# Two pairs of batches share one inverse iteration, and both head groups share what follows their scores

## The chip, the cores and the metric

The kernel runs on one core of a Trainium2 chip. The metric is the device time of one execution in microseconds (us); lower is better. The core has five engines with queues of their own: TensorE (PE in the profile, its weight loads PEld), VectorE (DVE), ScalarE (ACT), GpSimd (POOL) and SyncE (SP), which here issues all the DMAs.

## The reference

The kernel computes a Nystrom attention over 8 batches of 8 heads, 576 tokens and 64 channels, and a gated MLP on its output (4608 tokens, width 512, hidden width 1536). Everything is float32.

```python
q_lm, k_lm = means of q and k over 18 neighbouring tokens   # 32 landmarks per head
A  = sm(q, k_lm)        # 576 x 32
Bm = sm(q_lm, k_lm)     # 32 x 32
C  = sm(q_lm, k)        # 32 x 576
Z = Bm.T / (norm1(Bm) * norminf(Bm) + 1e-06)
for _ in range(6):
    Z = 2 * Z - Z @ Bm @ Z
attn = A @ Z @ C @ v
x = attn as (4608, 512);  xn = x / rms(x) * rms_g
out = (silu(xn @ w_gate) * (xn @ w_val)) @ w_out
```

`sm` is a scaled softmax over the last axis. The six steps of the iteration on Z depend on one another.

## The kernel before, in words

A float32 product is made from high and low parts: a large matmul of the MLP becomes three (high by high, high by low, low by high). The 8 heads of a batch are two groups `g` of four heads; a group fills the 128 partitions with four blocks of 32 landmarks.

**Attention, per batch b.** `stage1(b, g)` (line 335) sums q and k over 18 tokens (lmT, line 342), issues the loads of the next group's q and k and of its v (lines 347 and 348), and makes the scores sC, sA and B with small matmuls, their softmax for C and B (E, eb, Bm) and the transposed scores tA (line 395). `back()` (line 404), one for each group, follows some units later: the softmax of A on tA (lines 405 to 414), the transposed result AT and its parts AS, five transposes of E on TensorE (sE, sF), their copies ET and EL, and 20 small matmuls pCV of C by v, scaled into PV. `newton(b)` (line 459) does the inverse iteration for both groups of one batch: some preparation on DVE, p0 (8 matmuls of 32x32 blocks), five steps of pn (8 matmuls each) followed by one DVE instruction (line 498), a sixth pn into VZ (line 502), and pW (8 matmuls), split into Whi and Wlo. Steps carry Z and Z C v together. `second(b)` (line 539) multiplies W by AS (pO, 12 matmuls a group), copies pO into xr on ACT and squares it (sq), sums the squares with matmuls (pss, transposed on DVE, then pms), takes the reciprocal root with small DVE instructions (lines 571 to 581), spreads it (Rb, Rt), scales xr (line 587), stores xr to DRAM for the later passes (line 591), and `finish` splits xr into xhi and xlo (lines 614 and 616).

**MLP.** Tokens go in chunks of 512. `mlp_chunk(i)` (line 252) runs 144 large matmuls on the first four of twelve blocks of the hidden width: for each block 12 into psg and 12 into psv, silu and the product into h, then pso. The other eight blocks follow in two later passes over all tokens. A chunk of 512 tokens is not a batch of 576: chunk i needs x of batch i (its last part in `finish(i - 1, 1)`) before its first matmul.

**What sets the order.** All matmuls and transposes are held in program order, and a planner, `Mixer` (line 212), writes that order. Each piece of attention is a generator that yields a cost and a due time: `yield cost, wait` moves the planner's clock by the cost and makes the piece due again after wait times slack (1.3 once chunk 0 has begun). `fill` (line 239) moves the clock by 0.216 for each MLP matmul and then runs at most one due piece of attention. After the 144 matmuls of chunk i, `drain` (line 244) runs what is left, with no MLP matmul between, until `second(i + 1)` is done (line 690). Pieces start when their gates open (lines 638 to 660): `newton(b)` when the scores of b are done, and its steps after both `back()` of b; `second(b)` when newton(b) is done and chunk b - 1 has begun; the second half of `stage1(b)` when `second(b - 2)` is done, its first half when `newton(b - 2)` is. Chunks 7 and 8 and the later passes come after all attention. On the other engines a scheduler orders instructions by priority; `second` and `newton` go first.

**Buffers that the change touches.** PSUM has eight banks: three for the MLP, five (`pa`) for attention. E and tA have two buffers (one per group), xr has two, v two.

Of the kernel before, what the change touches and what calls it, by code (L numbers as in the profile page):

```python
# [18 lines left out]
P = 128  # L19
# [10 lines left out]
BW = 5.0  # L30
# [19 lines left out]
TAB = 2  # L50
# [25 lines left out]
TINY = 1.0513759e-09  # L76


@with_exitstack
def nystrom_moe_kernel(  # L80
# [47 lines left out]
    VZ = cst.tile([P, G, 3 * D], F32, name="VZ")  # L128
# [169 lines left out]
    with tc.tile_pool(name="ap", bufs=1, side="right") as ap, tc.tile_pool(  # L298
# [36 lines left out]
        def stage1(b, g):  # L335
            nt = state[b]
            qk = loaded.pop((b, g))
            vt, vl_ = loaded.pop((b, g, "v"))
# [7 lines left out]
            if b > 0 and nxt[0] < B:  # L346
                load_qk(*nxt)
                load_v(*nxt)
# [25 lines left out]
            rs = sm.tile([P, 2], F32, name="rs", tag="rs")  # L374
# [5 lines left out]
            E = ap.tile([P, S], F32, name="E", tag="E", bufs=2)  # L380
# [11 lines left out]
            (nc.scalar.mul if BMA else nc.vector.tensor_scalar_mul)(nt["Bm"][:, g, :], eb, rs[:, 1:2])  # L392
            tA = ap.tile([P, NB, M], F32, name="tA", tag="tA", bufs=TAB)
            for e in range(2):
                nc.vector.transpose(
                    tA[:, e * (NB // 2) : (e + 1) * (NB // 2), :].rearrange("p n m -> p (n m)"),
                    sA[e],
                )
            yield 1.3, 0.0
            if g == 1:  # L400
                stage["front"] = b

            def back():
                yield -BW * mix.slack
                mA = sm.tile([P, NB], F32, name="mA", tag="mA")
                nc.vector.tensor_reduce(mA, tA, axis=AX.X, op=ALU.max)
                nc.gpsimd.tensor_sub(tA, tA, mA.unsqueeze(2).broadcast_to([P, NB, M]))
                nc.scalar.activation(tA, tA, AF.Exp, scale=SC)
                sumA = sm.tile([P, NB], F32, name="sumA", tag="sumA")
                nc.vector.tensor_reduce(sumA, tA, axis=AX.X, op=ALU.add)  # L410
                nc.vector.tensor_scalar_add(sumA, sumA, 1e-9)
                rA = sm.tile([P, NB], F32, name="rA", tag="rA")
                nc.vector.reciprocal(rA, sumA)
                nc.gpsimd.tensor_mul(tA, tA, rA.unsqueeze(2).broadcast_to([P, NB, M]))
                AT = ap.tile([P, S], F32, name="AT", tag="AT", bufs=ATB)
                nc.vector.transpose(AT, tA.rearrange("p n m -> p (n m)"))
                AS = ap.tile([P, 2, S], F32R, name="AS", tag="AS", bufs=ASB)
                nc.scalar.copy(AS[:, 0], AT)
                nc.vector.tensor_sub(AS[:, 1], AT, AS[:, 0].bitcast(F32))
                nt["AT"][g] = AS  # L420

                sE = pa.tile([P, 4, P], F32, name="sE", tag="pa")
                for ch in range(4):
                    tp(sE[:, ch], E[:, ch * P : (ch + 1) * P], ident)
                sF = pa.tile([2 * M, P], F32, name="sF", tag="pa")
                tp(sF, E[:, 4 * P :], ident)
                ET = ap.tile([P, 4, P], F32, name="ET", tag="ET", bufs=ETB)
                EL = ap.tile([2 * M, P], F32, name="EL", tag="EL", bufs=ETB)
                nc.scalar.copy(ET, sE)
                nc.scalar.copy(EL, sF)  # L430
                yield 0.65, SW2
                pCV = pa.tile([P, D], F32, name="pCV", tag="pa")
                for ch in range(5):
                    for h in range(4):
                        r = slice(h * M, (h + 1) * M)
                        mm(
                            pCV[r, :],
                            ET[:, ch, r] if ch < 4 else EL[:, r],
                            vt[:, h, ch, :] if ch < 4 else vl_[:, h, :],
                            start=(ch == 0),  # L440
                            stop=(ch == 4),
                        )
                (nc.scalar.mul if CVA else nc.vector.tensor_scalar_mul)(nt["PV"][:, g, M:], pCV, rs[:, 0:1])
                yield 0.85, 0.2
                done[b] = done.get(b, 0) + 1
                if done[b] == 2:
                    stage["first"] = b

            mix.add(back())

        def bmm(lt, rhs, n, nm):
            ps = pa.tile([P, 2, n], F32, name=nm, tag="pa")
            for g in range(2):
# [5 lines left out]
        def newton(b):  # L459
            nt = state[b]  # L460
            Bm = nt["Bm"]
            BT = sm.tile([P, 2, M], F32, name="BT", tag="BT", bufs=1)
# [3 lines left out]
            sums = sm.tile([P, 4], F32, name="nsum", tag="nsum")  # L466
            nc.vector.tensor_reduce(
                sums[:, 0:2], Bm, axis=AX.X, op=ALU.add, apply_absolute_value=True
            )
            nc.vector.tensor_reduce(  # L470
                sums[:, 2:4], BT, axis=AX.X, op=ALU.add, apply_absolute_value=True
            )
            sb = sm.tile([P, 4, M], F32, name="nsb", tag="nsb", bufs=1)
            nc.vector.tensor_copy(sb, sums.unsqueeze(2).broadcast_to([P, 4, M]))
            sbt = sm.tile([P, 4, M], F32, name="nsbt", tag="nsbt", bufs=1)
# [3 lines left out]
            nm = sm.tile([P, 4], F32, name="nnm", tag="nnm")  # L479
            nc.vector.tensor_reduce(nm, sbt, axis=AX.X, op=ALU.max)  # L480
            den = sm.tile([P, 2], F32, name="nden", tag="nden")
            nc.vector.tensor_mul(den, nm[:, 0:2], nm[:, 2:4])
            nc.vector.tensor_scalar_add(den, den, 1e-6)
            nc.vector.reciprocal(den, den)
            Bs = sm.tile([P, 2, M], F32, name="Bs", tag="Bs")
            nc.vector.tensor_mul(Bs, Bm, den.unsqueeze(2).broadcast_to([P, 2, M]))
            PV = nt["PV"]
            yield 0.0, NW
            p0 = bmm(BT, BT, M, "p0")
            nc.vector.tensor_mul(PV[:, :, :M], p0, den.unsqueeze(2).broadcast_to([P, 2, M]))  # L490
            yield 0.35, 0.0
            while stage["first"] < b:
                yield -0.3
            yield 0.0, NS
            for _ in range(5):
                pn = bmm(PV[:, :, :M], PV, M + D, "pn")
                PVn = sm.tile([P, 2, M + D], F32, name="PV", tag="PV", bufs=3)
# [5 lines left out]
                VZ[:, :, D : 2 * D], PV[:, :, M:], 2.0, pn, op0=ALU.mult, op1=ALU.subtract  # L503
            )
            yield 0.45, NP
            Whi = sm.tile([P, 2, P], F32R, name="Whi", tag="Whi", bufs=1)
            Wlo = sm.tile([P, 2, P], F32R, name="Wlo", tag="Wlo", bufs=1)
            pW = pa.tile([P, 2, P], F32, name="pW", tag="pa")
            for g in range(2):
# [12 lines left out]
            nt["W"] = Whi, Wlo  # L522
            yield 0.5, WW

        def new_state(b):
            state[b] = {
                "Bm": sm.tile([P, 2, M], F32, name="Bm", tag="Bm"),
                "PV": sm.tile([P, 2, M + D], F32, name="PV", tag="PV", bufs=3),
                "AT": [None, None],
            }  # L530

        def first(b):
            new_state(b)
            for g in range(2):
                yield from stage1(b, g)
# [3 lines left out]
        def second(b):  # L539
            nt = state.pop(b)  # L540
            (Whi, Wlo), ATs = nt["W"], nt["AT"]
            xr = ap.tile([P, NK, S], F32, name="xr", tag="xr", bufs=2)
# [511 lines left out]
```

## Time and profile before

| | us |
|---|---|
| median of 3 runs (1065.81 to 1072.3) | 1068.71 |
| the profiled execution's own time | 1064.71 |
| its span, first to last instruction | 1062.8 |
| TensorE busy | 992.8 |
| DVE busy | 743.4 |
| ACT busy | 486.7 |
| POOL busy | 89.5 |

The profile is of one execution. Its busy times are sums over instructions, where pipelined matmuls overlap and their ends are modelled. A name such as `psg<-xhi,whig` gives the tile written and the tiles read, with buffer numbers left out. All matmuls carry line 141 (the helper `mm`) and the transposes line 144, so they are told apart by tile. A note in brackets after an instruction gives the idle time of its engine just before it and what ended it. The granted clock is that of TensorE, as a share of full speed.

### The profile page before, as it was taken

The page shows a single profiled execution, that of the slowest core. Times are in us where ns is not written, and L with a number is a line of the kernel's source. Part 1 is how long each engine was busy: PE and PEld are TensorE (multiplying, and loading weights), DVE is VectorE, ACT ScalarE, POOL GpSimd, SP SyncE. Part 2 cuts the span into 40 slices and gives each one's busy share as a digit, 9 for nine tenths or more (in the row PEclk, how much of TensorE's full clock was granted, in tenths as well). Part 3 has the DMA queues.
Part 4 walks back from the last instruction along what each step waited for, and adds up shares of the span by engine and source line. Part 5 has one row for each costly group of instructions (what it writes and reads, how often), then busy time and mean ns, then how long its engine had stood idle before and what let it go on. Part 6 is the DMA issues. An engine that isn't in the chain of part 4 may idle for free.

```text
span 1062.8 us, 17582 instructions
## 1 busy us (share of the span) xinstructions
PE 992.8 (93%) x6918; PEld 833.9 (78%) x6918; DVE 743.4 (70%) x1503; ACT 486.7 (46%) x990; POOL 89.5 (8%) x86
## 2 busy tenths in 40 slices
PE   5639689989989999999999999999999999999998
PEld 3326466556767777787989899998999989899997
DVE  7799586797494551988995675747897475675743
ACT  3534556555454543455645352433744334352431
POOL 2243121211020210100000000000000000000000
PEclk7659889999999999999999999999999999999999
DMA  9244343434140211543533505134250432505122
GB/s 335 100 150 136 133 164 105 153 104 163 43 142 11 86 45 40 187 145 119 189 123 135 178 1 179 51 129 155 64 178 21 159 96 83 179 1 178 50 70 80
DMA packets 62946, 123.82 MB, mean 117 GB/s; under 512 B 5520, under 2 KB 27024, under 8 KB 61840
## 3 DMA queue, kind: packets, MB, share of 16 engines
q1 hardware_dynamic: 62864, 122.71, 34.0%
q8 instruction: 54, 0.88, 0.3%
q14 instruction: 28, 0.23, 0.1%
HBM read 84.94 MB, written 37.75 MB: 115 GB/s over the span
## 4 chain that ended last, share of the span: by engine, by line
PE 72%; DVE 15%; DMA 6%; issue 2%; ACT 2%; POOL 2%; SPq 0%; ACTq 0%; POOLq 0%; DVEq 0%
PE pso L141 23%; PE px L141 18%; PE pz L141 9%; PE psg L141 6%; PE psv L141 5%; PE pw L141 5%; DMA qk<-in_q_dram 2%; PE pO L141 2%; DMA srawv<-in_moe_w_val_dram 1%; DVE lmT L342 1%; PE pn L141 1%; DVE xr L587 1%; DVE h L275 1%; PE sC L141 1%; PE pss L141 1%
## 5 line engine op out<-in xcount | busy, mean ns | idle before, releaser
L141 PE MATMUL pso<-whio,h 128*128 128x512 f32 x288 | 96.2, 402 | 5.8 <-DVE h L275 4.7
L141 PE MATMUL pso<-solo,h 128*128 128x512 f32 x432 | 100.4, 390 | 0.0
L829 ACT CAST x<-xf 128x768 fp32r<-128x768 f32 x84 | 68.1, 833 | 69.7 <-DVE xf L847 54.2
L141 PEld LDWEIGHTS pso<-solo,h 128*128 128x128 f32 x432 | 81.0, 188 | 16.3
L141 PE MATMUL pso<-sowhio,h 128*128 128x512 f32 x288 | 90.9, 390 | 0.0
L141 PE MATMUL psg<-xhi,whig 128*128 128x512 f32 x144 | 60.7, 421 | 25.6 <-ACT xhi L614 25.6
L945 DVE TENSOR_TENSOR ob<-ob,pso 128x512 f32<-128x512 f32 x72 | 48.8, 684 | 49.1 <-PE pso L141 48.1
L830 DVE TENSOR_TENSOR x<-xf,x 128x768 fp32r<-128x768 f32 x84 | 79.2, 953 | 5.0 <-ACT x L829 5.0
L877 DVE TENSOR_TENSOR h<-c,h 128x384 fp32r<-128x384 f32 x96 | 53.2, 555 | 37.3 <-ACT h L876 37.2
L898 ACT COPY c<-px 128x384 f32<-128x384 f32 x48 | 23.1, 481 | 108.6 <-PE px L141 108.6
L141 PEld LDWEIGHTS pso<-whio,h 128*128 128x128 f32 x288 | 53.4, 188 | 20.4 <-DVE h L275 6.0
L876 ACT CAST h<-c 128x384 fp32r<-128x384 f32 x96 | 49.4, 515 | 34.5 <-DVE c L887 28.3
L141 PE MATMUL psg<-xlo,whig 128*128 128x512 f32 x144 | 60.6, 421 | 4.7 <-DVE xlo L616 4.0
L141 PEld LDWEIGHTS pso<-sowhio,h 128*128 128x128 f32 x288 | 54.1, 188 | 11.0
L141 PE MATMUL psg<-xhi,wlog 128*128 128x512 f32 x144 | 60.5, 420 | 0.0
L141 PE MATMUL psv<-xhi,wlov 128*128 128x512 f32 x144 | 58.1, 403 | 0.0
L141 PE MATMUL px<-x,swfs0c 128*128 128x384 f32 x288 | 58.0, 335 | 0.0
L141 PE MATMUL psv<-xlo,whiv 128*128 128x512 f32 x144 | 58.0, 403 | 0.0
L141 PE MATMUL px<-x,swfs1c 128*128 128x384 f32 x288 | 57.8, 334 | 0.1
L141 PE MATMUL px<-x,swfs2c 128*128 128x384 f32 x288 | 57.8, 335 | 0.0
L141 PE MATMUL psv<-xhi,whiv 128*128 128x512 f32 x144 | 57.8, 401 | 0.0
L141 PE MATMUL pso<-wloo,h 128*128 128x512 f32 x144 | 57.4, 398 | 0.0
(224 smaller groups left out, 2231.6 us busy)
## 6 DMA issues: line engine op xcount, KB each, us to landing
xd<-xr SPq DMA_DIRECT2D x8, 1152.0 KB, 4.3
pd<-ob SPq DMA_DIRECT2D x36, 256.0 KB, 2.1
xf<-xd SPq DMA_DIRECT2D x8, 1152.0 KB, 7.5
ob<-pd SPq DMA_DIRECT2D x36, 256.0 KB, 3.5
pe<-ob SPq DMA_DIRECT2D x36, 256.0 KB, 2.6
ob<-pe SPq DMA_DIRECT2D x36, 256.0 KB, 2.8
out_dram<-ob SPq DMA_DIRECT2D x36, 256.0 KB, 2.7
vt<-in_v_dram SPq DMA_DIRECT2D x16, 512.0 KB, 4.0
```

The costliest lines, as they stand in the source:

```text
L141: tc.keep_in_program_order(nc.tensor.matmul(*args, **kw))
L275: nc.vector.tensor_sub(h2, s, h1.bitcast(F32))
L342: nc.vector.tensor_reduce(lmT[:, z], qk[z].rearrange("p h (m c) -> p h m c", c=LM), axis=AX.X, op=ALU.add)
L587: last = nc.vector.scalar_tensor_tensor(xr[:, kk], xr[:, kk], gsb[:, kk : kk + 1], Rt, op0=ALU.mult, op1=ALU.mult)
L829: nc.scalar.copy(t[:, 0], src)
L830: nc.vector.tensor_sub(t[:, 1], src, t[:, 0].bitcast(F32))
L876: nc.scalar.copy(hi, s)
L877: nc.vector.tensor_sub(lo, s, hi.bitcast(F32))
L898: nc.scalar.copy(c1, px)
L945: nc.vector.tensor_add(ob, ob, bank.pop(t))
```

## The change

`back` becomes a function of its own that does one or both groups. For batches 0 and 1 it runs per group as before; for batches 2 to 7 it runs once, after the scores of both groups, with instructions twice as wide and the matmuls of both groups one after the other (10 transposes, then 40 pCV). It loads v of the next batch when its pCV are issued; scores load only q and k from then on. `newton` takes a group of batches: (0), (1), (2), (3, 4), (5, 6), (7). For a pair, each p0, pn and pW is 16 matmuls, and each DVE instruction is twice as wide; it starts when the scores of the later batch are done and waits for that batch's back(). Scores of batch b now wait for `second(b - 2)` as a whole. E and tA are one buffer of both groups instead of one for each; xr has one buffer instead of two. Two new waits (SW3 2.6 before the 40 pCV, BW2 5.5 before a double back) stand beside the old ones.

```diff
-TAB = 2
+TAB = 1
+XRB = 1
+GROUPS = ((0,), (1,), (2,), (3, 4), (5, 6), (7,))
+BOTH = 2
+SW3 = 2.6
+BW2 = 5.5
...
             if b > 0 and nxt[0] < B:
                 load_qk(*nxt)
-                load_v(*nxt)
+                if nxt[0] <= BOTH:
+                    load_v(*nxt)
...
+            if g == 0:
+                nt["E"] = ap.tile([P, 2, S], F32, name="E", tag="E", bufs=1)
+                nt["tA"] = ap.tile([P, 2, NB, M], F32, name="tA", tag="tA", bufs=TAB)
+                nt["rs"] = sm.tile([P, 2, 2], F32, name="rs", tag="rs")
+                nt["AS"] = ap.tile([P, 2, 2, S], F32R, name="AS", tag="AS", bufs=2)
...
+            if b < BOTH:
+                mix.add(back(b, nt, g, 1))
+            elif g == 1:
+                mix.add(back(b, nt, 0, 2))
+
+        def back(b, nt, g0, n):
+            gs = range(g0, g0 + n)
+            gsl = slice(g0, g0 + n)
+            yield -(BW if n == 1 else BW2) * mix.slack
+            ta = nt["tA"][:, gsl]
+            tA = ta.rearrange("p g n m -> p (g n) m")
...
+            nc.vector.tensor_reduce(mA, tA, axis=AX.X, op=ALU.max)
+            nc.gpsimd.tensor_sub(tA, tA, mA.unsqueeze(2).broadcast_to([P, n * NB, M]))
+            nc.scalar.activation(tA, tA, AF.Exp, scale=SC)
...
+            for g in gs:
                 sE = pa.tile([P, 4, P], F32, name="sE", tag="pa")
                 for ch in range(4):
+                    tp(sE[:, ch], nt["E"][:, g, ch * P : (ch + 1) * P], ident)
+                nc.scalar.copy(ET[:, g], sE)
+            sF = pa.tile([2 * M, 2, P], F32, name="sF", tag="pa")
+            for g in gs:
+                tp(sF[:, g], nt["E"][:, g, 4 * P :], ident)
+            nc.scalar.copy(EL[:, gsl], sF[:, gsl])
+            yield 0.65 * n, SW2 if n == 1 else SW3
+            pCV = pa.tile([P, 2, D], F32, name="pCV", tag="pa")
+            for g in gs:
+                vt, vl_ = loaded.pop((b, g, "v"))
...
+            if n == 2 and b + 1 < B:
+                for g in range(2):
+                    load_v(b + 1, g)
+            yield 0.85 * n, 0.2
...
-        def newton(b):
-            nt = state[b]
+        def newton(group):
+            nt = state[group[0]]
+            n = 2 * len(group)
...
-            while stage["first"] < b:
+            while stage["first"] < group[-1]:
                 yield -0.3
...
-            xr = ap.tile([P, NK, S], F32, name="xr", tag="xr", bufs=2)
+            xr = ap.tile([P, NK, S], F32, name="xr", tag="xr", bufs=XRB)
...
         def firsts():
             for b in range(1, B):
-                while stage[GATE0 if b > 2 else G2] < b - (1 if b == 2 else 2):
+                while stage["newton"] < b - 2 or (b == 2 and stage["newton"] < 1):
+                    yield -0.3
+                while b > 2 and stage["second"] < b - 2:
                     yield -0.3
                 new_state(b)
-                yield from stage1(b, 0)
-                while stage[GATE1] < b - 2:
-                    yield -0.3
-                yield from stage1(b, 1)
+                for g in range(2):
+                    yield from stage1(b, g)
 
         def newtons():
-            for b in range(B):
-                while stage["front"] < b:
+            for group in GROUPS:
+                while stage["front"] < group[-1]:
                     yield -0.3
-                yield from newton(b)
-                stage["newton"] = b
+                yield from newton(group)
+                stage["newton"] = group[-1]
```

More of the change, by code (lines that the diff above doesn't have):

```diff
@@ L127, in nystrom_moe_kernel @@
     nc.vector.memset(ones, 1.0)
-    VZ = cst.tile([P, G, 3 * D], F32, name="VZ")
+    VZ = cst.tile([P, 2 * G, 3 * D], F32, name="VZ")
     nc.gpsimd.memset(VZ, 0.0)
@@ L401, in stage1 @@
                 stage["front"] = b
[L403 to L420, printed above, removed]
+            if b < BOTH:
+                mix.add(back(b, nt, g, 1))
+            elif g == 1:
+                mix.add(back(b, nt, 0, 2))
@@ L422, in back @@
                 sE = pa.tile([P, 4, P], F32, name="sE", tag="pa")
                 for ch in range(4):
[L424 to L430, printed above, removed]
@@ L436, in back @@
                         mm(
-                            pCV[r, :],
-                            ET[:, ch, r] if ch < 4 else EL[:, r],
+                            pCV[r, g, :],
+                            ET[:, g, ch, r] if ch < 4 else EL[:, g, r],
                             vt[:, h, ch, :] if ch < 4 else vl_[:, h, :],
@@ L442, in back @@
                         )
[L443 to L449, printed above, removed]
+            at = nt["at"]
+            nc.vector.tensor_mul(
+                nt["PV"][:, at + g0 : at + g0 + n, M:], pCV[:, gsl], nt["rs"][:, gsl, 0:1].broadcast_to([P, n, D])
+            )
+            if n == 2 and b + 1 < B:
+                for g in range(2):
+                    load_v(b + 1, g)
+            yield 0.85 * n, 0.2
+            done[b] = done.get(b, 0) + n
+            if done[b] == 2:
+                stage["first"] = b
         def bmm(lt, rhs, n, nm):
-            ps = pa.tile([P, 2, n], F32, name=nm, tag="pa")
-            for g in range(2):
+            w = lt.shape[1]
+            ps = pa.tile([P, w, n], F32, name=nm, tag="pa")
+            for g in range(w):
                 for h in range(4):
@@ L502, in newton @@
             nc.vector.scalar_tensor_tensor(
-                VZ[:, :, D : 2 * D], PV[:, :, M:], 2.0, pn, op0=ALU.mult, op1=ALU.subtract
+                VZ[:, :n, D : 2 * D], PV[:, :, M:], 2.0, pn, op0=ALU.mult, op1=ALU.subtract
             )
             yield 0.45, NP
[L506 to L509, printed above, removed]
+            Whi = sm.tile([P, 4, P], F32R, name="Whi", tag="Whi", bufs=1)[:, :n]
+            Wlo = sm.tile([P, 4, P], F32R, name="Wlo", tag="Wlo", bufs=1)[:, :n]
+            pW = pa.tile([P, n, P], F32, name="pW", tag="pa")
+            for g in range(n):
                 for h in range(4):
@@ L521, in newton @@
             nc.vector.tensor_sub(Wlo, pW, Whi.bitcast(F32))
-            nt["W"] = Whi, Wlo
+            for b in group:
+                state[b]["W"] = Whi, Wlo
             yield 0.5, WW
         def new_state(b):
[L526 to L535, printed above, removed]
+            group = next(gr for gr in GROUPS if b in gr)
+            if b == group[0]:
+                tiles = {
+                    "Bm": sm.tile([P, 4, M], F32, name="Bm", tag="Bm", bufs=1),
+                    "PV": sm.tile([P, 4, M + D], F32, name="PV", tag="PV", bufs=3),
+                }
+                for i, c in enumerate(group):
+                    state[c] = dict(tiles, at=2 * i)
         state = {}
@@ L550, in second @@
                             cols = slice(e * HS, (e + 1) * HS)
-                            mm(po[e][j], w[r, g], ATs[g][r, a, cols], start=(n == 0), stop=(n == 2))
+                            mm(po[e][j], w[r, at + g], AS[r, a, g, cols], start=(n == 0), stop=(n == 2))
                 for e in range(2):
```

63 lines of the change are left out of this document (37 added, 26 removed).

## The prediction

> **What bounds the kernel now.** I read the page first, then the busy times by stage, then the order of work on the TensorE queue.
>
> ```profile
> span 1062.8 us, 17582 instructions
> PE 992.8 (93%) x6918; PEld 833.9 (78%) x6918; DVE 743.4 (70%) x1503; ACT 486.7 (46%) x990; POOL 89.5 (8%) x86
> ...
> PEclk7659889999999999999999999999999999999999
> ```
>
> Four stages (columns: stretch, length, busy time and count of each engine, granted clock, DMA):
>
> ```profile
> 67.00:122.40 55.40, 51.60 (x477) 36.15 (x477) 39.92 (x69) 27.54 (x58) 18.21 (x13) 0.91 0.41 131
> 122.40:142.40 20.00, 6.93 (x21) 5.24 (x21) 20.00 (x56) 8.70 (x21) 6.02 (x6) 0.57 0.39 145
> 142.40:437.00 294.60, 281.58 (x2780) 201.00 (x2778) 194.30 (x489) 146.33 (x315) 47.84 (x45) 0.99 0.27 95
> 437.00:1062.80 625.80, 619.99 (x3196) 571.19 (x3196) 433.23 (x749) 277.87 (x534) 0.37 (x1) 1.00 0.35 115
> ```
>
> From 142 us on TensorE sets the time: it is idle for 13.0 us of the 294.6 in which attention is woven into the MLP, while DVE works 194 us of it. Everything after 437 us is MLP alone and is not touched. So an edit counts by the TensorE work it saves there and by the TensorE idle time it opens. Apart from the start of chunk 0, the one long hole is the change from chunk 0 to chunk 1:
>
> ```profile
> 122.40 0.40 PE L141 MATMUL pms<-sqT,sel 128*128 128x18 f32 x2
> 134.06 0.79 PE L141 MATMUL psg<-xhi,whig 128*128 128x512 f32 x1 [11.26 <-ACT xhi L614]
> ...
> 137.73 0.80 PE L141 MATMUL psg<-xlo,whig 128*128 128x512 f32 x1 [1.82 <-DVE xlo L616]
> ```
>
> There the sum of squares of batch 1 is the last thing on the queue before chunk 1, and chunk 1 needs that batch's normalised x. At chunk 2 the same step has MLP matmuls behind it, and little is left of the hole:
>
> ```profile
> 193.45 0.29 PE L141 MATMUL pms<-sqT,sel 128*128 128x18 f32 x2
> ...
> 200.59 0.50 PE L141 MATMUL psg<-xhi,whig 128*128 128x512 f32 x1 [0.44 <-ACT xhi L614]
> 201.90 0.50 PE L141 MATMUL psg<-xlo,whig 128*128 128x512 f32 x1 [0.81 <-DVE xlo L616]
> ```
>
> **The order after the change.** The matmuls stay in program order, and the planner fixes that order from its own costs (0.216 per MLP matmul, the costs and due times in the yields). This is used for order and counts only. Worked through for the old code it puts pms of batch 1 next to chunk 1 and that of batch 2 with MLP work behind it, as the rows show. For the new code it gives four things.
>
> 1. Scores of batch 4 may not start before second(2) is done, and W of batch 3 now waits for batch 4. Chunk 1 therefore runs out of its 144 matmuls before pss of batch 2: pss, pms and the normalisation stand bare before chunk 2.
> 2. In chunk 2 come scores 4.0, 4.1, back(4), and newton(3, 4) up to its fifth pn. Then the fillers are used up. The last pn, pW, both pO groups, pss, pms and the normalisation of batch 3 stand bare before chunk 3, which needs that x.
> 3. In chunk 4, newton(5, 6) and second(5) end late: pms of batch 5 has 10 MLP matmuls behind it. Chunks 4, 6 and 7 start covered.
> 4. Chunks 0 and 1 start as before.
>
> **Price of a bare normalisation.** The rows of batch 7, whose own cover hides them, give the steps:
>
> ```profile
> 420.94 1.18 PE L141 MATMUL pss<-sq,ones 128*32 128x288 f32 x16
> 421.75 0.92 DVE L563 STREAM_TRANSPOSE sqT<-pss 128x288 f32<-128x288 f32 x2 [0.83 <-PE pss L141]
> ...
> 424.49 0.29 PE L141 MATMUL pms<-sqT,sel 128*128 128x18 f32 x2
> ...
> 424.82 0.18 DVE L571 TENSOR_SCALAR ms<-pms 128x18 f32<-128x18 f32 x1 [2.15 <-PE pms L141]
> 425.03 0.18 DVE L575 TENSOR_SCALAR r<-ms 128x18 int32<-128x18 int32 x1
> ...
> 428.26 0.46 DVE L583 TENSOR_SCALAR Rb<-r 128x576 f32<-128x576 f32 x1
> ...
> 429.57 3.07 DVE L587 SCALAR_TENSOR_TENSOR xr<-xr,gsb,Rt 128x576 f32<-128x576 f32 x4
> ```
>
> Pss end (422.12) to transposes end (422.67) 0.55; pms to DVE 0.33 and 0.1 before it; 11 small steps at 0.21 (424.82 to 425.03) 2.3; Rb to xr 1.3; xr 3.1; the first xlo about 0.5: 8.2 us from pss to steady MLP matmuls, 7.5 from pms. Row check: 193.45 to 201.90 is 8.45, with other DVE work between.
>
> After such a hole the clock is low:
>
> ```profile
> 235.00:240.00 5.00, 1.84 (x40) 0.71 (x35) 5.00 (x8) 1.57 (x4) 1.83 (x2) 1.00 0.72 265
> 240.00:245.00 5.00, 5.00 (x61) 3.14 (x58) 3.38 (x11) 2.01 (x4) 0.92 (x1) 0.66 0.84 298
> ```
>
> A stop of 3.2 us cost 5 x (1 - 0.66) = 1.7 us of TensorE afterwards; I take 1.7 to 2.0 for each hole. The Trainium skill (TensorE: Matmul & The Clock Gate, What's actually happening) says that the half clock comes after a whole idle window of about 3.4 us that runs free; by that the 4.8 us hole of term C would hold such a window in some 4 of 10 cases and its 1.7 would be 0.7 on the mean, an estimate that lowers the sum by 1.
>
> **A, before chunk 2:** pss 1.2 + 8.2 = 9.4, less TensorE's own work in it (pss, pms, one psg: 1.6), plus 1.8: **+9.6**. Low end 7.5; high end from chunk 1's hole: 122.40 to 137.73 is 15.3, less 1.3, plus 2: 16.
>
> **B, before chunk 3.** The only bare Newton end is batch 0's:
>
> ```profile
> 37.54 0.65 PE L141 MATMUL pn<-PV 32*32 32x64 f32 x16 [1.26 <-DVE PV L498]
> ...
> 46.63 2.01 PE L141 MATMUL pss<-sq,ones 128*32 128x288 f32 x16
> ```
>
> Last pn to end of pss 11.1 us, at a low clock. Two batches in pn and pW add about 1 us; fewer other instructions take about as much off. So 10.7 + 8.2 = 18.9. TensorE's own work in it, at 0.47 per eight pn (158.03 to 158.50 below), and pW and one group of pO by
>
> ```profile
> 168.00:169.00 1.00, 0.64 (x16) 0.37 (x16) 0.00 (x0) 0.16 (x1) 1.00 0.00 0
> ```
>
> ```profile
> 177.50:178.70 1.20, 1.07 (x12) 0.83 (x12) 0.43 (x2) 1.00 0.00 0
> ```
>
> is 0.9 + 1.3 + 2.1 + 1.6 = 5.9; with the clock's 2.0, 18.9 - 5.9 + 2.0: **+15.0**. Ends 12 and 25 (low: a last pn that need not wait, and 9 instead of 10.7 to the end of pss; high: DVE as crowded as at 122 us adds 7, waits for PSUM banks 3).
>
> **C, before chunk 5:** 7.5 less ten fillers at 0.23 and 0.4 of own work, plus 1.7: **+6.5**. Ends 2 (1.3 as at 200.59, and no clock loss) and 10.
>
> **D, one xr buffer.** Copies of pO(4) and pO(6) stand one or two matmuls behind a chunk's start and wait until the previous xr is stored:
>
> ```profile
> xd<-xr SPq DMA_DIRECT2D x8, 1152.0 KB, 4.3
> ...
> vt<-in_v_dram SPq DMA_DIRECT2D x16, 512.0 KB, 4.0
> ```
>
> On ACT the silu and the evacuation of pso queue behind them; on TensorE the second pO group, some 13 fillers later, waits for its banks: **+2** together, ends 0 and 8. The v loads move behind pCV of the batch before, on SP's queue ahead of later q, k and p stores; the next reader, pCV of the next batch, comes at least 16 units of the plan later, where an MLP matmul is 0.216, which hides 4.0 us: 0, or 4 each if that cover were gone.
>
> **E, one E and one tA buffer, three PSUM tiles in a row in back().** Scores 6.0 precede back(5) in the order and hold four of five attention banks until it has read E and tA. Nearest rows:
>
> ```profile
> 217.95 0.30 PE L144 MATMUL sF<-ident,E 128*64 128x128 f32 x1 [0.68 <-ACT ET L429]
> ```
>
> ```profile
> 239.88 0.43 PE L141 MATMUL sA<-qk,lmT 64*32 64x288 f32 x1 [3.16 <-DVE PV L443]
> ```
>
> Two waits like the first and some of the second: **+2**, ends 0 and 6.
>
> **G, fewer turns between small and large matmuls.** Eight pn between two fillers:
>
> ```profile
> 157.62 0.48 PE L141 MATMUL psv<-xhi,whiv 128*128 128x512 f32 x1
> 158.03 0.53 PE L141 MATMUL pn<-PV 32*32 32x96 f32 x16
> 158.50 0.50 PE L141 MATMUL psv<-xlo,whiv 128*128 128x512 f32 x1
> 158.84 0.40 PE L141 MATMUL psv<-xhi,wlov 128*128 128x512 f32 x1
> ```
>
> 157.62 to 158.84 is 1.22 for two fillers worth 0.46: 0.76 per visit. A double visit has eight more pn, about 0.4, so it saves 0.35. Two pairs x (p0, 6 pn, pW) = 16, of which 14 lie among fillers: 4.9. Six batches x (transposes, pCV) = 12 at 0.3: 3.6. **-8.5**, ends -4 and -12.
>
> **H, old stalls.** Of the 13.0 us, those of chunk 2's start and of waiting banks go, with their low clock, while silu waits stay: **-7**, ends 0 and -16.
>
> Sum: 9.6 + 15.0 + 6.5 + 2 + 2 - 8.5 - 7 = +19.6. The profiled execution took 1064.7 (span 1062.8), so 1084.3; the median of the runs, 1068.7, stands 4.0 above it. I forecast **1087 us**, between carrying that offset over wholly and not.
>
> The wider PV step of a pair is costed at nothing: at 352 ns for 192 columns and 286 for 128 (rows below) it takes some 0.55 us for 384, 0.2 more, beside five fillers of 0.23 that follow each pn in the order. With that cover gone, ten steps would cost 2 us. The planner's waits of newton for the later batch of its pair hold up no engine by themselves; what is late next is second() of the earlier batch, and that is terms B and C.
>
> **Rivals.**
> *The holes are as dear as the early ones.* Chunk 1's 16 us instead of 9.6, B at 25, C at 10, D and E at 10, G and H at -10: +51, so 1105 to 1120. For it: DVE is busy for all of 122 to 142. Against it: the new holes have no weights to decode and no scores beside them.
>
> *DVE's fixed cost was on the path.* Widths 192 and 128 differ little (columns: count, shortest, median and longest ns, first and last start):
>
> ```profile
> L498 DVE SCALAR_TENSOR_TENSOR PV<-PV,pn x30: 310/352/355, 157.2 to 370.2; 128x192 f32<-128x192 f32 x30
> ...
> L502 DVE SCALAR_TENSOR_TENSOR VZ<-PV,pn x6: 247/286/289, 167.3 to 372.7; 128x128 f32<-128x128 f32 x6
> ```
>
> 352 - 286 over 64 elements leaves 0.15 us per instruction that does not scale. Two Newtons (18 instructions each) and six backs (7 each) fall away: 78 x 0.15 = 12 us of DVE. If that frees the queue where scores and PV wait, H reaches -16 and A, B, C their low ends: 7.5 + 12 + 2 + 0 - 8.5 - 16 = -3, so 1062 to 1066, not slower; it decides once H and G pass -21. For it: DVE is 5.00 of 5 busy in 235 to 240. Against it: 100 of 295 us free on DVE. [...]
>
> *The order is not as worked out,* so no hole opens: G, H and E alone, -13.5, 1051 to 1057. Against it: the old order comes out as the trace has it.
>
> **How the numbers follow.** Forecast (1074 to 1104) 0.66; dear holes (1104 to 1120) 0.14; DVE 0.13, half of it within 0.5% of the old median and half below that, since its 1062 to 1066 straddles 1063.4; no holes 0.07. A change of under 0.5%, 1063.4 to 1074.1, cannot be told from none. Faster 0.11, same 0.09, slower 0.80. The range 1066 to 1107 leaves out 0.1 on either side.
>
> **What would show it.** Two new waits of psg for ACT xhi at the starts of chunks 2 and 3 of 7 us and more, a third of some 4 us at chunk 5, each followed by a clock near 0.5 to 0.8; between the last fillers of chunk 2 and chunk 3's first, pn, pW, pO, pss, pms with nothing between; 32 pn instructions in one visit. Absent holes at chunks 2 and 3, or MLP matmuls between batch 3's pO and pms, would prove me wrong; a stage from chunk 7 on that differs by more than 3 us would be a cause that I have not seen.

## The result and the profile after

The changed kernel takes **1097.82 us** (median of 4 runs, 1096.17 to 1100.58), the kernel before 1068.56 us in the runs beside it (1065.81 to 1072.3). The ratio is 1.0274, with a 95% interval of 1.0236 to 1.0312: the change makes the kernel slower by 29 us. The forecast was 1087 us with a range of 1066 to 1107 and a chance of 0.80 for slower, so the direction was right and the time lies inside the range, 11 us above the forecast.

The profiled execution took 1097.15 us, with a span 32.3 us longer than before's. First the head of its page:

```profile
span 1095.1 us, 17452 instructions
...
PE 999.6 (91%) x6918; PEld 844.6 (77%) x6918; DVE 740.9 (68%) x1425; ACT 488.5 (45%) x974; POOL 88.8 (8%) x74
```

TensorE has the same 6918 matmuls and shows 6.8 us more busy time, although there are fewer turns between small and large matmuls: part of it now runs at half clock. DVE has 78 instructions fewer, as counted in the prediction, but only 2.5 us less work. The busy times by stage, of the changed kernel (stretch, length, busy time and count of PE, PEld, DVE, ACT and POOL, granted clock, DMA share, GB/s; the marks are pms of batch 1, the start of steady work in chunk 1, and the start of chunk 7):

```profile
120.80:144.60 23.80, 6.24 (x24) 4.57 (x16) 21.55 (x55) 7.32 (x18) 8.36 (x6) 0.57 0.35 128
144.60:476.70 332.10, 295.19 (x2812) 216.28 (x2811) 200.80 (x428) 153.93 (x311) 45.96 (x35) 0.93 0.25 89
476.70:1095.10 618.40, 613.41 (x3169) 565.82 (x3167) 425.90 (x733) 273.44 (x527) 0.00 (x0) 1.00 0.34 114
```

The same stretches of the kernel before, from steady chunk 1 on:

```profile
142.40:443.60 301.20, 288.08 (x2809) 206.36 (x2807) 200.81 (x504) 149.41 (x323) 48.22 (x46) 0.99 0.28 97
443.60:1062.80 619.20, 613.49 (x3169) 565.82 (x3167) 426.71 (x733) 274.79 (x527) 0.00 (x0) 1.00 0.34 114
```

Nearly all of the loss is in the woven stage, 332.1 us against 301.2. TensorE's idle time there grows from 13.1 to 36.9 us, and its clock falls from 0.99 to 0.93. The hole before steady chunk 1 grows by 3.8 us (20.0 before); what stands ahead of it is 1.6 us shorter, and from chunk 7 on 0.8 us shorter. DVE's busy time in the stage is the same to 0.01 us.

**The holes before chunks 2, 3 and 5.** The timeline of TensorE in the changed kernel, around the starts of chunks 2, 3 and 5 (start, length of the group, engine, line, operation, and in brackets the idle time before it with what ended it):

```profile
192.48 0.39 PE L146 MATMUL pso<-whio,h 128*128 128x512 f32 x1
192.79 1.18 PE L146 MATMUL pss<-sq,ones 128*32 128x288 f32 x16
194.58 0.40 PE L146 MATMUL pms<-sqT,sel 128*128 128x18 f32 x2 [0.60 <-DVE sqT L590]
200.07 0.79 PE L146 MATMUL psg<-xhi,whig 128*128 128x512 f32 x1 [5.10 <-ACT xhi L641]
203.35 0.79 PE L146 MATMUL psg<-xlo,whig 128*128 128x512 f32 x1 [2.49 <-DVE xlo L643]
...
208.21 0.63 PE L146 MATMUL psv<-xhi,whiv 128*128 128x512 f32 x1
...
251.36 0.65 PE L146 MATMUL pn<-PV 32*32 32x64 f32 x32
252.56 1.08 PE L146 MATMUL pW<-VZ,Bs 32*32 32x128 f32 x32 [0.54 <-DVE VZ L530]
...
259.77 2.66 PE L146 MATMUL pss<-sq,ones 128*32 128x288 f32 x14 [1.67 <-ACT sq L583]
263.01 0.62 PE L146 MATMUL pms<-sqT,sel 128*128 128x18 f32 x2 [0.58 <-DVE sqT L590]
268.73 0.80 PE L146 MATMUL psg<-xhi,whig 128*128 128x512 f32 x1 [5.11 <-ACT xhi L641]
...
271.98 0.80 PE L146 MATMUL psg<-xlo,whig 128*128 128x512 f32 x1 [0.71 <-DVE xlo L643]
...
276.84 0.63 PE L146 MATMUL psv<-xhi,whiv 128*128 128x512 f32 x1
...
377.02 0.39 PE L146 MATMUL pso<-whio,h 128*128 128x512 f32 x1
379.96 0.80 PE L146 MATMUL psg<-xhi,whig 128*128 128x512 f32 x1 [2.55 <-ACT xhi L641]
383.17 0.80 PE L146 MATMUL psg<-xlo,whig 128*128 128x512 f32 x1 [2.41 <-DVE xlo L643]
...
388.53 0.39 PE L146 MATMUL psv<-xhi,whiv 128*128 128x512 f32 x1
```

The order is the one worked out: before chunk 2, pss, pms and the normalisation stand bare; before chunk 3 the last pn (32 matmuls in one visit), pW, both groups of pO, pss and pms follow one another with no MLP matmul between; before chunk 5 ten MLP matmuls stand behind pms (the last at 377.02). Each hole is measured from its first bare instruction to the thirteenth large matmul of the new chunk, less what this work takes at full clock (0.23 for a large matmul; the prediction's rows for the rest):

- Chunk 2: 192.79 to 208.21 is 15.4; pss 1.2, pms 0.3 and twelve psg 2.7 are 4.2; lost **11.2 us**.
- Chunk 3: 251.36 to 276.84 is 25.5; pn 0.8, pW 1.1, three groups of pO 3.2, pss 1.2, pms 0.3 and twelve psg 2.7 are 9.3; lost **16.2 us**.
- Chunk 5: 377.25 to 388.53 is 11.3; one group of pO and twelve psg are 3.8; lost **7.5 us**.

**The banks of batches 5 and 6.** TensorE and ACT of the changed kernel around back(5) and the scores of batch 6, and then three stretches after a stop (columns as in the stages):

```profile
300.64 1.16 ACT L427 ACTIVATE tA<-tA 128x1152 f32<-128x1152 f32 x1
...
301.82 1.28 ACT L275 ACT_TABLE_LOAD   x1
...
303.61 0.58 ACT L446 COPY ET<-sE 128x512 f32<-128x512 f32 x1
...
304.24 0.66 PE L149 MATMUL sE<-ident,E 128*128 128x128 f32 x4 [1.98 <-ACT ET L446]
...
305.57 0.64 PE L149 MATMUL sF<-ident,E 128*64 128x128 f32 x2 [0.68 <-ACT ET L446]
...
317.91 0.67 PE L146 MATMUL sC<-qk,lmT 64*32 64x288 f32 x2 [2.72 <-DVE rs L402]
```

```profile
305.00:310.00 5.00, 4.42 (x12) 3.52 (x13) 5.00 (x10) 2.41 (x6) 1.23 (x2) 0.50 0.18 72
317.00:329.00 12.00, 11.09 (x61) 8.50 (x62) 11.33 (x25) 4.62 (x10) 2.14 (x1) 0.86 0.51 179
200.00:208.50 8.50, 5.94 (x13) 4.37 (x14) 5.51 (x7) 2.55 (x9) 4.02 (x4) 0.50 0.34 139
```

The second set of transposes waits for the copy ET, which stands on ACT behind the now twice as wide exponential of A, a load of ACT's tables and a silu. The waits are 5.4 us, and the clock afterwards costs 5.0 x 0.50 + 12.0 x 0.14 = 4.2: **9.6 us** together, a little low, since the first spell at half clock runs on to about 311.6. The third stretch is the one after the hole of chunk 2.

**Newton of batch 7.** Steps of the sixth Newton in the changed kernel, with what DVE does ahead of them:

```profile
420.87 0.28 DVE L466 TENSOR_TENSOR PV<-pCV,rs 128x128 f32<-128x128 f32 x1
421.07 2.35 DVE L643 TENSOR_TENSOR xlo<-xr,xhi 128x448 fp32r<-128x448 f32 x1
421.20 0.53 PE L146 MATMUL pn<-PV 32*32 32x96 f32 x16 [0.80 <-DVE PV L466]
...
423.33 1.37 DVE L435 STREAM_TRANSPOSE AT<-tA 128x1152 f32<-128x1152 f32 x1
...
425.00 0.53 PE L146 MATMUL pn<-PV 32*32 32x96 f32 x16 [1.89 <-DVE PV L526]
...
427.60 0.53 PE L146 MATMUL pn<-PV 32*32 32x96 f32 x16 [0.72 <-DVE PV L526]
```

The longest of the three waits, 1.89 us, is for a DVE instruction of 0.31 us (line 526) that stands behind an xlo of 2.35 and a wide transpose of 1.37. The first is for PV out of pCV (line 466), and ahead of the third DVE does another wide instruction (AS, 1.36). The three waits are **3.4 us**.

**The start of chunk 1.** Its first matmul waits 14.80 us for xhi (11.26 before) and the first xlo 2.75 (1.82):

```profile
136.00 0.80 PE L146 MATMUL psg<-xhi,whig 128*128 128x512 f32 x1 [14.80 <-ACT xhi L641]
139.55 0.79 PE L146 MATMUL psg<-xlo,whig 128*128 128x512 f32 x1 [2.75 <-DVE xlo L643]
```

In the 14.8 us, DVE now does more other work between the small steps of the normalisation of batch 1, wide reductions for batch 2 and sums lmT:

```profile
125.94 1.35 DVE L425 TENSOR_REDUCE mA<-tA 128x36 f32<-128x1152 f32 x1
...
127.36 1.34 DVE L347 TENSOR_REDUCE lmT<-qk 128x64 f32<-128x1152 f32 x1
...
131.15 1.34 DVE L429 TENSOR_REDUCE sumA<-tA 128x36 f32<-128x1152 f32 x1
```

where the kernel before had, in the same place, reductions of one group, such as:

```profile
125.04 0.74 DVE L410 TENSOR_REDUCE sumA<-tA 128x18 f32<-128x576 f32 x1
```

The wide reductions are the smaller part of the difference. The two of them (1.35 and 1.34) stand against two of one group (0.74 and 0.73), 1.2 us more; but three sums lmT of some 1.34 us lie within this wait, where one did before, 2.7 us more.

### The profile page after: what moved, and what is told of

Read it like the earlier page. It is cut to its first block, busy times and chain, and to the rows that moved or that the text cites. A ratio compares the mean times of both kernels' runs of the same rounds, so it can differ in the third digit from the quotient of the medians.

```text
span 1095.1 us, 17452 instructions
## 1 busy us (share of the span) xinstructions
PE 999.6 (91%) x6918; PEld 844.6 (77%) x6918; DVE 740.9 (68%) x1425; ACT 488.5 (45%) x974; POOL 88.8 (8%) x74
## 4 chain that ended last, share of the span: by engine, by line
PE 47%; DVE 9%; DMA 3%; ACT 1%; issue 1%; SPq 0%; ACTq 0%; DVEq 0%
PE pso L146 17%; PE px L146 16%; PE pz L146 8%; PE pw L146 4%; DMA srawg<-in_moe_w_gate_dram 1%; DVE x L857 1%; DMA srawo<-in_moe_w_out_dram 1%; DVE sw L759 1%; PE psg L146 1%; PE psv L146 1%; DVE sw L762 1%; DVE h L280 1%; DMA pe<-ob 1%; ACT sw L754 1%; DVE sw L755 1%
## 5 line engine op out<-in xcount | busy, mean ns | idle before, releaser
L904 DVE TENSOR_TENSOR h<-c,h 128x384 fp32r<-128x384 f32 x96 | 53.3, 555 | 37.0 <-ACT h L903 36.9
L146 PEld LDWEIGHTS psg<-xhi,whig 128*128 128x128 f32 x144 | 29.4, 204 | 49.5 <-ACT xhi L641 42.3
```

The costliest lines, as they stand in the source:

```text
L146: tc.keep_in_program_order(nc.tensor.matmul(*args, **kw))
L904: nc.vector.tensor_sub(lo, s, hi.bitcast(F32))
```

## The experiments

My theory was the prediction's: the loss is the bare normalisations that the new order opens (pairs first, then the scores that go before back()). The rivals were that the wide back() or the single buffers of E, tA and xr cost the time, that pairing itself does, and that some other wait takes the place of whatever is removed. All runs keep the whole computation. The ratios are to the kernel before, with 95% intervals.

| run | what of the change it has | us | ratio |
|---|---|---|---|
| whole change | all | 1097.82 | 1.0274 [1.0236, 1.0312] |
| e1_back_only | double back(), no pairs | 1079.41 | 1.0107 [1.0082, 1.0132] |
| e2_pairs_only | both pairs, back() per group | 1095.55 | 1.0258 [1.0233, 1.0283] |
| e3_buffers_only | buffers and gate alone | 1067.2 | 0.9992 [0.9975, 1.0009] |
| e4_early_scores | all, scores a batch earlier | 1098.92 | 1.0299 [1.0266, 1.0332] |
| e5_pairs_late | pairs (4, 5), (6, 7), covered | 1068.42 | 1.0001 [0.9986, 1.0017] |
| e6_singles_same_plan | as e5, no pairs | 1063.31 | 0.9953 [0.9936, 0.9969] |
| e7_pair_34 | pair (3, 4) alone | 1087.04 | 1.0175 [1.0154, 1.0195] |
| e8_pair_56 | pair (5, 6) alone | 1076.41 | 1.0071 [1.0050, 1.0093] |
| e9_back_sooner | all, back() sooner | 1097.4 | 1.0273 [1.0253, 1.0293] |
| e10_pairs_late_act | as e5, PV scaled on ACT | 1062.29 | 0.9939 [0.9922, 0.9956] |
| e11_singles_act | as e6, PV scaled on ACT | 1063.79 | 0.9964 [0.9944, 0.9983] |
| e12_back_sooner_act | as e9, PV scaled on ACT | 1089.36 | 1.0204 [1.0169, 1.0239] |

### Which part costs the time

e1 takes the pairs out, e2 the double back(), e3 both, so that only the single buffers of E, tA and xr and the gate on the whole batch stay:

```diff
# e1
-GROUPS = ((0,), (1,), (2,), (3, 4), (5, 6), (7,))
+GROUPS = ((0,), (1,), (2,), (3,), (4,), (5,), (6,), (7,))
# e2
-BOTH = 2
+BOTH = 8
# e3: both edits
```

> Every batch has its own newton again; both head groups still share back() from batch 2 on, with the single E, tA and xr buffers. Theory O (the loss is bare stretches that the order leaves on TensorE): in this order only pms of batch 2 stands bare before chunk 2 (about 7.5 us plus 2 of low clock), all later chunks are covered by 16 planner units or more, and 12 turns are saved; so 1072 to 1079, with one new wait of psg for ACT xhi of some 5 us and none at chunk 3 or 5. Theory W (the wider back() and its single buffers lose the time: the bank waits at back(5), 9.7 us with their low clock, the later start of chunk 1, 3.8 us, and the waits of newton(7) behind wide DVE instructions, 3.4 us): these stay and recur in other batches, so 1083 to 1092.

> Batches 3+4 and 5+6 share the iteration; back() runs for each group alone in all batches; E, tA and xr stay in the shared single buffers. Theory O: pms of batch 2 bare before chunk 2 (9 us), pO to the normalisation of batch 3 bare before chunk 3 (about 15), pms of batch 5 with 4.5 planner units behind it (4 to 5), 14 turns saved (4.6): 1085 to 1093, with the holes at chunks 2, 3 and 5. Theory W: most of the 29 us goes with the wide back(): 1070 to 1080.

> No pair and no shared back(): what is left of the change is the shared single E and tA buffers, the single xr buffer and the scores that wait as a whole for second() two batches before. Theory O: the order has no bare stretch, pms of batch 2 has 2.2 planner units behind it (3 to 5 us at chunk 2): 1069 to 1075. Theory S (the single buffers alone lose time, since scores of a batch hold four PSUM banks until back() of the batch before has read E and tA): 1080 or more, with waits of sA, sC or sE for banks.

The buffers and the gate cost nothing on balance that can be measured (0.9992, the interval holds 1). They do move waits: e3 waits 2.72 and 2.21 us for xhi and xlo at chunk 2 (0.44 and 0.81 before), and the old wait of 3.16 us at sA is gone. The pairs alone cost 27 us and the double back() alone 11. Against the theory's ranges e1 and e2 end 0.4 and 2.6 us too high and e3 1.8 too low; none reaches its rival's. The two costs sum to more than the whole, because both parts open the hole of chunk 2: in e1 psg waits there 5.10 and 2.48 us, in e2 5.10 and 2.49, in the whole change 5.10 and 2.49. The longer wait of chunk 1 belongs to the double back() (14.03 and 2.76 in e1, with three sums lmT in it; 11.28 and 1.82 in e2, as before, with one), the hole of chunk 3 to the pairs (5.11 in e2, no such wait in e1). Both have a wait besides at a pn for PV, line 466: 6.43 us in e1, 3.20 in e2.

### Which pair

e7 and e8 leave one pair each, with back() per group:

```diff
# e7
+GROUPS = ((0,), (1,), (2,), (3, 4), (5,), (6,), (7,))
# e8
+GROUPS = ((0,), (1,), (2,), (3,), (4,), (5, 6), (7,))
# both
+BOTH = 8
```

> Only the pair (3, 4), back() for each group alone, all other gates as changed. Theory O: pms of batch 2 bare before chunk 2 (about 9 us), pO to the normalisation of batch 3 bare before chunk 3 (15 to 17 us), 7 turns saved (2.3 us), old stalls less: 22 to 27 us above e3, 1089 to 1094, nearly all of e2's loss. Theory P: the two pairs cost alike, so 1078 to 1083.

> Only the pair (5, 6), otherwise as e7. Theory O: by the plan pms of batch 5 stands with no MLP matmul behind it before chunk 5; with DVE free there that is 8 to 10 us of hole, less 2.3 for the turns: 6 to 8 above e3, 1073 to 1076. Theory P: 1078 to 1083.

Against e3, the pair (3, 4) costs 20 us and the pair (5, 6) 9; together 29, and e2 with both stands 28 above e3. So the pairs add up. e7 is 2.0 us below the theory's range and e8 0.4 above; neither is in the rival's. e7 shows the holes of chunks 2 and 3 (5.10 and 2.48; 1.67 at pss, 5.11 and 0.72) and none at chunk 5; e8 shows one at chunk 5 and none at chunks 2 and 3 beyond e3's own. That ties each hole to its pair. TensorE's timeline of e8 at chunk 5:

```profile
358.77 0.79 PE L146 MATMUL psg<-xhi,whig 128*128 128x512 f32 x1 [4.94 <-ACT xhi L641]
```

### Giving the holes cover

If the loss is the missing MLP matmuls, scores that may start a batch earlier should give Newton, and then the normalisation, something to stand behind. e4 is the whole change with one gate moved:

```diff
-                while b > 2 and stage["second"] < b - 2:
+                while b > 2 and stage["second"] < b - 3:
```

> The whole change, but scores of batch b wait for second(b - 3) instead of second(b - 2), so batches 4 and 6 start earlier. Theory O: batch 3's last pn, pW and pO get MLP matmuls again; bare stay pms of batch 2 (9 us instead of 11.4) and pss and pms of batch 3 (11 instead of 17), and the hole at chunk 5 (7.5) goes: 16 us less than the changed kernel, 1079 to 1085. Theory W or S: scores now precede back() of the batch before more often, the bank waits grow, and the time stays at 1090 or more.

That was a miss: no gain at all. Newton and pO of batch 3 were covered, as meant, but pms of batches 2 and 3 still stood bare, and now with the scores of the next batch beside it. The timeline of TensorE, DVE and POOL of this run at chunk 2:

```profile
205.44 2.13 POOL L433 TENSOR_TENSOR tA<-tA,rA 128x1152 f32<-128x1152 f32 x1 [6.21 <-DVE rA L432]
205.49 2.11 DVE L606 SCALAR_TENSOR_TENSOR r<-r,ms 128x18 f32<-128x18 f32 x1
...
212.32 0.79 PE L146 MATMUL psg<-xhi,whig 128*128 128x512 f32 x1 [16.23 <-ACT xhi L641]
```

The same bare normalisation costs a wait of 5.1 us where DVE has nothing else, and 16.2 where lmT, mA, sumA and the preparation of Newton stand between its small steps (14.43 at chunk 3). Some 3.8 of these 11.1 us more are two small steps that took 1.99 and 2.11 us, each beside a wide GpSimd instruction. What the Newton of batch 3 gained in cover, the two normalisations lost again in DVE's queue.

### Pairs that are covered

e5 moves the pairs one batch later, with the early gate, back() per group, and a shorter wait ahead of pss; e6 is the same without pairs:

```diff
# both
-OWL = 7.0
+OWL = 5.0
+BOTH = 8
+                while b > 2 and stage["second"] < b - 3:
# e5
+GROUPS = ((0,), (1,), (2,), (3,), (4, 5), (6, 7))
# e6
+GROUPS = ((0,), (1,), (2,), (3,), (4,), (5,), (6,), (7,))
```

> Pairs (4, 5) and (6, 7) instead of (3, 4) and (5, 6), back() for each group alone, scores of b wait for second(b - 3), and the wait before pss is 5 units instead of 7 (OWL). By the plan no chunk starts bare: behind pms stand 7.2 units before chunk 2 and 19 or more before all later chunks. Theory O: pairing costs nothing where its chain is covered and saves 16 turns of 0.33 us, so 4 to 6 us less than the same kernel without pairs (e6), and 1060 to 1067 in all. Theory P (pairing itself loses time, by longer steps and wider DVE instructions in the queue): 5 us or more above e6.

> As e5 without any pair: the price of the plan's other edits (early scores, shorter wait before pss). Theory O: 7.2 units behind pms of batch 2 leave at most 2 us at chunk 2, so 1063 to 1070; if early scores crowd DVE at the bare chunk starts as in e4, 1072 to 1080.

The holes at later chunks are gone in e5, at chunk 2 waits of 1.88 and 2.79 us are left (2.00 and 3.02 in e6), and with the holes goes the loss: 1.0001 against 1.0258 for the earlier pairs. That part of the theory stands. But the gain expected from fewer turns did not come, and e5 ends above its range; e6 without pairs is 5 us faster than e5, which is what theory P named, and faster than the kernel before (0.9953). It differs from e3 in the gate and in the wait ahead of pss; I did not separate these two. e5 had two waits that e6 had not, on TensorE, and DVE's queue shows why:

```profile
250.77 0.37 PE L146 MATMUL pn<-PV 32*32 32x96 f32 x8 [3.71 <-DVE PV L466]
...
297.69 3.46 DVE L614 SCALAR_TENSOR_TENSOR xr<-xr,gsb,Rt 128x576 f32<-128x576 f32 x4
...
303.68 0.21 DVE L466 TENSOR_TENSOR PV<-pCV,rs 128x64 f32<-128x64 f32 x1
303.95 1.11 PE L149 MATMUL sE<-ident,E 128*128 128x128 f32 x4 [5.48 <-DVE PV L466]
```

The 0.21 us in which PV is scaled out of its PSUM tile wait behind the scaling of xr and the xlo of another batch and what DVE does after them, and transposes that need a bank wait for it. e10 and e11 take these 0.21 us off DVE:

```diff
-            nc.vector.tensor_mul(
-                nt["PV"][:, at + g0 : at + g0 + n, M:], pCV[:, gsl], nt["rs"][:, gsl, 0:1].broadcast_to([P, n, D])
-            )
+            for g in gs:
+                nc.scalar.mul(nt["PV"][:, at + g, M:], pCV[:, g], nt["rs"][:, g, 0:1])
```

> The pairs (4, 5) and (6, 7) of the run before with its late gates, with PV scaled from pCV on ACT, one instruction a group, instead of on DVE. Theory V (what the covered pairs lost is PV standing on DVE behind the normalisation: waits of 3.71 at pn and 5.48 at sE, with the low clock some 10 to 13 us): both waits fall under 1 us and the time is 1056 to 1062 us. Rival (the loss is POOL and DVE being slow together, or the plan of the pairs itself): about 1068 us, with the waits at other tiles.

> The same order without pairs (1063.3 us), also with PV scaled on ACT. It had no wait on PV above 1.6 us. Theory V: 1060 to 1064 us, and the kernel with pairs is then faster than this one by the turns that it saves, 4 to 6 us. Rival (pairs gain nothing even where covered): this one is as fast as the kernel with pairs or faster.

Both waits go (the largest at pn is now 1.40 us, at sE 1.10), and the kernel with covered pairs becomes 6 us faster, 1062.29 us. Both waits and the time stay just above what was named (under 1 us, and 1056 to 1062). The kernel without pairs does not change beyond its interval. So the wait for PV was what e5 had lost. The pairs' own gain stays open: 1.5 us between e10 and e11, with intervals that overlap, where 4 to 6 were expected. In the stretch from chunk 2 to chunk 7 the two are equal (232.84 and 232.10 us), although e10 has 15 visits of attention fewer; it has 1.4 us more idle time there, and a clock of 0.98 against 0.99.

The clock shows where most of the saving went. In e10, two stops follow each other closely, 1.10 us at sE and 1.54 at sF (297.60), and after them the clock is 0.50 from 297 to 303; e11 has no such spell between 212 us and chunk 7 (1.00). That spell costs some 2.9 us. With the idle time it is 4.3 of the 5.0 that 15 visits at 0.33 us should save (an estimate; the 0.33 is worked out in the next section).

e6, e10 and e11 beat both kernels of this case, and cannot be told from one another.

### The term of the banks

e9 lets back() go ahead of the next scores, to test whether the 9.6 us at batches 5 and 6 come from scores that hold the banks; e12 scales PV on ACT as well, with the edit above:

```diff
-BW2 = 5.5
+BW2 = 4.0
```

> The whole change, but the wait ahead of a double back() is 4.0 instead of 5.5, so that back(5) stands ahead of the scores 6.0 in the order. Theory E (scores that go first hold banks and leave TensorE on the copies ET and on rs, 9.7 us with the low clock after it): the waits of 1.98, 0.68 and 2.72 us at sE, sF and sC of batches 5 and 6 go, and the hole before chunk 2 loses its pss; 1085 to 1090 us. Rival (the waits come from ACT and DVE being late there, whatever goes first): the time stays at 1095 or more, with waits of the same size at the same tiles.

> The whole change with the double back() ahead of the scores, as in the run that gave 1097.4 us, and PV scaled from pCV on ACT. That run had lost the waits of batches 5 and 6 in part (1.98, 0.68 and 2.72 us became 0.92, 2.27 and 1.06), and had a wait of 7.13 us at pn of batch 7 for PV, which stood on DVE behind the normalisation of batch 6. Theory V (what PV waits for is its place in DVE's queue): that wait falls under 1.5 us, its low clock goes with it, and the time is 1086 to 1091 us; the holes before chunks 2 and 3 stay as they are, 5.1 + 2.5 and 5.1 + 0.7 us at psg. Rival (the plan of the whole change has some such wait wherever one is removed): 1095 us or more, with a new wait of 4 us or more at another tile.

e9 was a miss in time. The waits at batches 5 and 6 changed from 1.98, 0.68 and 2.72 to 0.92, 2.27 and 1.06 us, the last two with no releaser that the profile shows, and a new one stood at the pn of batch 7:

```profile
416.88 0.86 PE L146 MATMUL pn<-PV 32*32 32x96 f32 x16 [7.13 <-DVE PV L466]
```

e12 is 8.0 us faster than e9. That pn does not wait any more, as theory V has it; the next one waits 1.85 us for PV of the step before (line 525), behind a wide transpose and xr on DVE. The holes of chunks 2 and 3 are as they were (5.09 and 2.49; 5.11 and 0.72). I count 13.0 us for batches 5 and 6 and for the Newton of batch 7 in the whole change. The time falls by 8.5 (1097.82 to 1089.36) when both the order and the place of PV are changed, and by nothing when the order alone is; which of the waits the 8.5 belong to was not taken apart. What PV on ACT is worth in the whole change without the other order was not tried. In what remains of the loss (1.0204) the holes of chunks 1, 2 and 3 stand as they did, and that of chunk 5 with waits of 1.64 and 2.71 us.

## Why the prediction was right, and where it was off

**What bounds the kernel** held: TensorE's idle time and clock in the woven stage make the result, and the stage from chunk 7 on differs by 0.8 us.

**The signs** came in part. The psg waits for xhi at chunks 2 and 3 were to be 7 us and more, and are 5.10 and 5.11: the prediction counted its 7.5 us to steady matmuls, and the first psg, which needs only xhi, starts before the last of xr is scaled. The rest follows as the wait for xlo (2.49 and 0.71). At chunk 5 the wait for xhi is 2.55 in place of some 4, with 2.41 for xlo. The half clock, the bare order before chunk 3 and the 32 pn in one visit are as named.

**The order** held in all four points, down to the ten matmuls behind pms of batch 5. e7 and e8 show that the holes follow the pairs.

| step | forecast | range | measured |
|---|---|---|---|
| start of chunk 1 | 0 | none | +3.8 |
| A, before chunk 2 | +9.6 | 7.5 to 16 | +11.2 |
| B, before chunk 3 | +15.0 | 12 to 25 | +16.2 |
| C, before chunk 5 | +6.5 | 2 to 10 | +7.5 |
| D, one xr buffer | +2 | 0 to 8 | 0 |
| E, one E and tA buffer, three PSUM tiles | +2 | 0 to 6 | +9.6 |
| Newton of batch 7 | not named | none | +3.4 |
| G and H, turns and old stalls | -15.5 | -4 to -28 | about -17 |

The last row is what is left over: the six measured losses sum to 51.7 us, the stretches ahead of chunk 1 and after chunk 7 are 1.6 and 0.8 shorter, and the span grew by 32.3. Part of it can be read directly: idle time in the stage is 36.9 us, of which 31.7 stand in the rows above, so 5.2 are left of the 13.1 of before. That is -7.9 for H, where -7 was forecast, without the low clock that followed those stalls. The other 9 are G with that clock, by subtraction only. For G's size by itself there are only the steps of the double Newton with five MLP matmuls between, in the changed kernel:

```profile
241.07 0.86 PE L146 MATMUL pn<-PV 32*32 32x96 f32 x32
...
243.22 0.86 PE L146 MATMUL pn<-PV 32*32 32x96 f32 x32
```

and of the single one before:

```profile
361.40 0.53 PE L141 MATMUL pn<-PV 32*32 32x96 f32 x16
...
363.21 0.53 PE L141 MATMUL pn<-PV 32*32 32x96 f32 x16
```

A period of 2.15 us against 1.81; with 1.14 for the five fillers a double visit costs 1.01 and two single ones 1.34: 0.33 saved, where 0.35 was forecast. In e10 against e11 this saving did not reach the end time: most of it went into one more spell of half clock and into idle time, as shown above.

**The terms that failed.**

- *E* was the largest: 9.6 us for a forecast of 2 with an upper end of 6. The step took two waits like an old one of 0.68 us and some of one of 3.16. It did not count that the copy ET queues on ACT behind a doubled exponential and a table load (1.16 and 1.28 us), nor that each stop is followed by half clock (4.2 of the 9.6). The mechanism named, scores first and banks held, is not shown to be more than a part of it: with back() first (e9), the waits there fell only from 5.4 to 4.3 us, and the time did not move until PV was off DVE too.
- *Chunk 1*: "Chunks 0 and 1 start as before" was right for the order and wrong for the price. The hole was bare already, so all that DVE does in it counts in full. With the double back() two more sums lmT (2.7 us) and the wide reductions (1.2 us more) stand there. e1 has the longer wait, e2 has not.
- *Newton of batch 7*: "The wider PV step of a pair is costed at nothing" looked at the step's own 0.2 us. What counts is what stands ahead of a short step on DVE: a wide transpose and a slow xlo, 3.4 us here; at PV out of pCV it is 6.43 and 7.13 in e1 and e9.
- *A, B and C* are each 1 to 1.6 us low. At chunk 2 two sizes show why. Scaling xr and the first xlo were put at 3.1 + 0.5 = 3.6 us and take 4.7: xr starts at 198.66 and takes 3.78, and the first xlo matmul starts at 203.35. And the low clock was taken at 1.7 to 2.0 us a hole, where twelve psg at 0.43 in place of 0.23 lose 2.4.
- *D* cost nothing: no pO or copy of pO waited for the single xr beyond half a microsecond, and e3 confirms it in time.

**The rivals.** That DVE's fixed cost on the path decides did not come true: 78 instructions went, and the time got longer. In the stage DVE is busy 200.80 us against 200.81. Single wide instructions do save what was worked out (a sum over tA takes 1.34 us for two groups against 0.74 for one), and other instructions took it back: the 24 xlo of the stage went from 14.0 to 19.6 us. Holes as dear as the early ones were right on one point only: e4 shows that they become so (16.2 and 14.4 us of wait) once scores stand beside them, and in the whole change they do not. The order was not other than worked out.

**The Trainium skill's rule on the clock** (TensorE: Matmul & The Clock Gate, What's actually happening) was weighed with term C: a half clock only after a whole idle window of some 3.4 us would have taken 1 us off the sum. The runs do not bear it out for this kernel: after two stops of 1.98 and 0.68 us with transposes between, the clock is 0.50 for the next 5 us. At chunk 5 it falls to 0.50 at about 380 us, after a stop of 2.55 us, and stays there to 386, so term C had its low clock in full. The stop of 3.16 us, after which the prediction read its 0.66, was itself shorter than such a window.

**The time.** The sum of terms gave 1084.3 for the profiled execution, which took 1097.15; in the span it was 19.6 against 32.3, 12.7 us off. E (+7.6), Newton of batch 7 (+3.4), chunk 1 (+3.8) and A, B and C (+3.8) were too low, 18.6 together; D (-2), G and H (some -1.5), and the two other stretches (-2.4) give back 5.9. The forecast of 1087 had added part of the offset between profiled execution and median, and so stands 11 below the median measured.

## What to carry to other kernels

When two pieces of work are merged, list not only the turns that this saves but when the merged piece now ends, and which consumer's cover is used up by then: here 33 visits of attention fewer (72 against 105 in the woven stage) saved some 9 us, by what is left over in the sum, and two bare chains cost 27. A bare chain of small steps has no price of its own; it costs what stands between its steps on the engine's queue, 5 us or 16 us of wait for the same instructions. Before widening instructions on a shared in-order engine, look for the shortest instruction that TensorE waits for behind them; moving one such step of 0.2 us to another engine was worth 6 and 8 us in the kernels that had such a wait, and nothing in one that had none.

## What the runs showed of the hardware

- **A small DVE instruction can last as long as a GpSimd instruction beside it.** In e4's rows above, the step r<-r,ms takes 2.11 us, where the same step takes 0.18 in the whole change at 195.86, with POOL idle; it starts 0.05 us after POOL's tA<-tA,rA of 2.13 us and ends with it. The Trainium skill states such an exclusive lock of a shared pair of ports, held for a whole instruction (SBUF — State Buffer, SBUF: two separate sides), and these rows agree. The wide POOL instructions of the double back() (2.13 us for two groups, against 1.16 for one) make one such stop twice as long.
- **Not every instruction is held.** In the whole change, DVE's xlo at 421.07 takes 2.35 us beside POOL's tA<-tA,rA (2.58 us from 420.35), but another xlo of the same shape, at 418.76, takes 0.61 us within a POOL instruction of 1.73 from 418.67. The profile's spans on POOL are rough, so what decides between the two is open.
